# Pooled attention and a two-matrix MoE block: the second product by the seven-product form at two levels instead of one

## The chip, the cores and the metric

The kernel runs on one core of a Trainium2 chip. The metric is the device time of one execution in microseconds (us), lower is better. A difference of 0.2% (about 2 us) is the smallest that a measurement of this kernel tells from no change. The engines are named as in the profile: PE (matrix products), PEld (its weight loads), DVE (vector), ACT (scalar and table functions), POOL and SP (which here issues all DMAs).

## The reference, cut to what matters

```python
# q, k, v: (8, 8, 576, 64) f32; k and v are averaged over blocks of 8 positions
attn = softmax(q @ k_p.T / sqrt(64));  x = attn @ v_p      # x as (4608, 512)
h = x @ w_in                                               # (4608, 2048)
s = sin(alpha * h)
g = h + s * s / (alpha + 1e-9)
out = g @ w_out                                            # (4608, 512), f32
```

Everything is float32. The last line, `g @ w_out`, is the second MoE product and what the change rewrites.

## The kernel before, in words

The work has two phases over nine units (`NU`) of 512 tokens each.

**Phase one.** For each unit, `hidden` computes `h` and `g` in four groups (J), each by the seven-product form of a 2x2 block product (Strassen's form in Winograd's variant: seven half-size products and some additions instead of eight products). A group has seven products of eight matmul records each, all 128x256 outputs. A float32 matmul appears in the trace as two records, each with its own weight load. Some products continue on the partial sum of another one: ACT copies a PSUM bank into the next (L320, L328) and the next product accumulates on the copy. ACT computes the sines and squares (L315, L336 and on), DVE adds (L310), and SP stores the group of `g` to `g_bridge` in HBM (L349). For the first seven units the attention of the next unit is interleaved. Beside unit 7, after which no attention is left, `load_w_out` (L252) loads `w_out` in four blocks of 1 MB (L259), scales its rows by 1/alpha (32 ACT operations of 128x256, L265) and forms the block sums that the seven-product form needs (16 DVE operations of 128x512, L267).

**Phase two.** For each unit, `load_g` reads the four groups of `g` back (L361, 1 MB each). `output` (L364) forms the block sums of `g` on DVE (L371, 16 operations of 128x512 a unit) and runs the seven products in the order 1, 4, 2, 6, 7, 5, 3. A product is 16 matmuls (32 records) with a 128x128 block of `g` as the loaded weights and a 128x256 block of `w_out` as the moving side (L384). Product 2 accumulates on product 1's bank and product 3 on product 5's. ACT copies (L395, L399, L401) and DVE adds (L391) combine the banks into the output tile, which SP stores in two halves (L418).

The tile framework's scheduler sets the order of the instructions on every engine; each engine then runs its own list in order, and waits on semaphores where another engine's or a DMA's result is needed. PSUM has eight banks; five are the pool `ps_m` that both phases use, three the attention's.

Of the kernel before, what the change touches and what calls it, by code (L numbers as in the profile page):

```python
# [36 lines left out]
class Kernel:  # L37
# [187 lines left out]
    def load_w_in(self):  # L225
# [25 lines left out]

    def load_w_out(self, wp):  # L252

        nc, h, kk = self.nc, self.DM // 2, self.K2 // 2
        blk = lambda n: wp.tile([P, kk, h], F32, name=n)
        b11, b12, b21, b22, t1, t2, t4 = (blk(n) for n in ("b11", "b12", "b21", "b22", "bt1", "bt2", "bt4"))
        src = self.w_out.rearrange("(k p) n -> p k n", p=P)
        for t, i, j in ((b11, 0, 0), (b12, 0, 1), (b22, 1, 1), (b21, 1, 0)):
            nc.sync.dma_start(out=t[:], in_=src[:, i * kk:(i + 1) * kk, j * h:(j + 1) * h])  # L259
        self.Bw = {1: b11, 2: b21, 3: b22, 4: t4, 5: t1, 6: t2, 7: b12}  # L260
        for c in range(0, kk, 2):
            for t, i in ((b11, 0), (b12, 0), (b22, 1), (b21, 1)):
                for k in range(c, c + 2):
                    f = i * kk + k
                    nc.scalar.mul(out=t[:, k], in_=t[:, k], mul=self.ral[:, f:f + 1])  # L265
            s = slice(c, c + 2)
            tt = lambda o, x, y: nc.vector.tensor_tensor(out=o[:, s], in0=x[:, s], in1=y[:, s], op=OP.subtract)  # L267
            tt(t1, b12, b11)
            tt(t2, b22, t1)
            tt(b12, b22, b12)  # L270

            tt(t4, b21, t2)
            yield

# [10 lines left out]
    def hidden(self, u, first):  # L285
# [12 lines left out]
        def product(p, J, ps, start):  # L298
            for jj in range(JW):
                f = J * JW + jj  # L300
                for kk in range(2):
                    nc.tensor.matmul(ps[:, jj, :], self.A[p][:, kk, f * P:(f + 1) * P], Bx[p][:, kk, :],  # L302
                                     start=(start and jj == 0 and kk == 0), stop=(kk == 1), skip_group_check=True)
# [50 lines left out]

    def load_g(self, u):
        g = []
        for J in range(self.NJ):
            t = self.gp.tile([P, 2, 2, JW, TH], F32, name="g")  # L360
            self.nc.sync.dma_start(out=t[:].rearrange("p a b c d -> p (a b c d)"), in_=self.gd[u, J])  # L361
            g.append(t)
        return g

    def output(self, u, g):
        nc = self.nc
        G = []
        for J in range(self.NJ):
            s = self.gs.tile([P, 4, JW, TH], F32, name="gs")
            A = lambda i, j: g[J][:, j - 1, i - 1]  # L370
            tt = lambda o, x, y, op: nc.vector.tensor_tensor(out=o, in0=x, in1=y, op=op)  # L371
            tt(s[:, 0], A(2, 1), A(2, 2), OP.add)
            tt(s[:, 1], s[:, 0], A(1, 1), OP.subtract)
            tt(s[:, 2], A(1, 1), A(2, 1), OP.subtract)
            tt(s[:, 3], A(1, 2), s[:, 1], OP.subtract)
            G.append({1: A(1, 1), 2: A(1, 2), 3: s[:, 3], 4: A(2, 2), 5: s[:, 0], 6: s[:, 1], 7: s[:, 2]})
        NT = TH // P
        hw = self.DM // 2

        def product(p, ps, start=True):  # L380
            for t in range(NT):
                for J in range(self.NJ):
                    for jj in range(JW):
                        nc.tensor.matmul(ps[:, t, :], G[J][p][:, jj, t * P:(t + 1) * P], self.Bw[p][:, J * JW + jj, :],  # L384
                                         start=(start and t == 0 and J == 0 and jj == 0), stop=(J == self.NJ - 1 and jj == JW - 1),
                                         skip_group_check=True)
        bank = lambda: self.ps_m.tile([P, NT, hw], F32, name="ps_m", tag="m")
        tmp = lambda n: self.op.tile([P, NT, hw], F32, name=n)
        o = self.op.tile([P, 2, NT, self.DM], F32, name="o")
        C = lambda i, j: o[:, i - 1, :, (j - 1) * hw:j * hw]  # L390
        add = lambda o, x, y: nc.vector.tensor_tensor(out=o, in0=x, in1=y, op=OP.add)  # L391
        b1 = bank()
        product(1, b1)
        p1 = tmp("p1")
        nc.scalar.copy(out=p1[:], in_=b1[:])  # L395
        b4 = bank()
        product(4, b4)
        p4 = tmp("p4")
        nc.scalar.copy(out=p4[:], in_=b4[:])  # L399
        product(2, b1, False)  # L400
        nc.scalar.copy(out=C(1, 1), in_=b1[:])  # L401
        b6 = bank()
        product(6, b6)
        u2 = tmp("u2")
        add(u2[:], p1[:], b6[:])
        b7 = bank()
        product(7, b7)
        u3 = tmp("u3")
        add(u3[:], u2[:], b7[:])
        add(C(2, 1), u3[:], p4[:])  # L410
        b5 = bank()
        product(5, b5)
        add(C(2, 2), u3[:], b5[:])
        product(3, b5, False)
        add(C(1, 2), u2[:], b5[:])
        for i in range(2):
            r = u * 2 * TH + i * TH
            nc.sync.dma_start(out=self.out[r:r + TH, :].rearrange("(t p) n -> p t n", p=P), in_=o[:, i])  # L418

    def run(self):  # L420
        nc, tc = self.nc, self.tc
        pool = lambda s, n, b, **kw: s.enter_context(tc.tile_pool(name=n, bufs=b, **kw))
        with ExitStack() as top:
            const = self.const = pool(top, "const", 1)
            self.tp = pool(top, "tp", 2)
            self.ps_m = pool(top, "ps_m", 5, space=PSUM)
            ident = self.ident = const.tile([P, P], F32, name="ident")
            make_identity(nc, ident)
            with ExitStack() as one:
                self.wp = pool(one, "wp", 1)  # L430
                self.hp = pool(one, "hp", 2)
                self.xp = pool(one, "xp", 2)
                att = one.enter_context(ExitStack())
                cb = pool(att, "cb", 1)
                self.kvp = pool(att, "kv", 3)
                self.qp = pool(att, "qp", 1)
                self.ap = pool(att, "ap", 1)
                self.sm = pool(att, "sm", 3)
                self.ps_a = pool(att, "ps_a", 3, space=PSUM)
                self.mark_banks()  # L440
                self.kblk = []
                for i in range(2):
                    t = cb.tile([P, self.NP, 2 * self.Sp], F32, name=f"kblk{i}")
                    nc.gpsimd.memset(t[:], 0.0)
                    self.kblk.append(t)
                st = self.load_batch(0)
                self.load_alpha()
                self.load_w_in()
                for _ in self.attention(0, st):
                    pass  # L450
                for u in range(self.NU):
                    nxt = iter(())
                    if u + 1 < self.B:
                        nxt = self.attention(u + 1, self.load_batch(u + 1))
                        steps = 48
                    elif u == self.B - 1:
                        att.close()
                        wo = pool(top, "wo", 1, side="right")
                        self.gp = pool(top, "gp", self.NJ, side="right")
# [10 lines left out]
                g = self.load_g(0)  # L470
            self.gs = pool(top, "gs", self.NJ)
            self.op = pool(top, "op", 2)
            for u in range(self.NU):
                self.output(u, g)
                if u + 1 < self.NU:
                    g = self.load_g(u + 1)


@with_exitstack
# [32 lines left out]
```

## Time and profile before

| What | Value |
|---|---|
| Time before, median of 3 runs | 1082.56 us (1081.94 to 1083.32) |
| The profiled execution's own time | 1081.14 us |
| Its span, first to last instruction | 1079.3 us (so 1.84 us lie around it) |
| Mean granted PE clock | 0.987 |
| PE / PEld / DVE / ACT / POOL busy | 1037.8 / 879.6 / 494.9 / 376.6 / 218.1 us |
| Matmul records / weight loads | 5288 / 5288 |
| HBM read / written | 75.51 MB / 47.19 MB |

How to read it: busy time is the time in which an engine has an instruction in flight. Matmuls are pipelined: consecutive records overlap, so the spacing of their starts, not the length of one, is what a stream costs. In a timeline row the columns are start, length, engine, line, operation, output and inputs, the shapes (weights, then the moving side), the count, and in brackets the engine's idle time before the row and who ended it. In a windows row each engine has its busy time and its count of instructions, then come the granted clock, the share of the 16 DMA engines that was busy, and GB/s.

### The profile page before, as it was taken

What the parts mean: (1) busy time and instruction counts of PE and PEld (TensorE: products, weight loads), DVE (VectorE), ACT (ScalarE), POOL (GpSimd) and SP (SyncE); (2) the same over time, 40 slices, a digit from 0 to 9 for tenths busy, and PEclk for the clock granted to TensorE, in tenths of its full rate; (3) what the DMA queues carried; (4) which work ended last, traced back from release to release, by engine and by line L of the source; (5) the groups of instructions that cost most, each with busy time, mean ns of one, the idle gap of its engine ahead of it and who ended that gap; (6) DMA issues with size and microseconds to landing.
All of it is one profiled execution on the core that took longest, in us unless ns stands there. A gap on an engine that the chain in (4) does not pass through costs nothing.

```text
span 1079.3 us, 13285 instructions
## 1 busy us (share of the span) xinstructions
PE 1037.8 (96%) x5288; PEld 879.6 (81%) x5288; DVE 494.9 (46%) x925; ACT 376.6 (35%) x682; POOL 218.1 (20%) x228
## 2 busy tenths in 40 slices
PE   6679999999999999999969999999999999999998
PEld 5467787878878888788758888888888888888886
DVE  4998573664636557464454251413133140413131
ACT  2246565565645757457486540000000000000000
POOL 4697870441705412002000000000000000000000
PEclk9799999999999999999989999999999999999999
DMA  7945461623516223110471213131332313131301
GB/s 172 242 116 151 147 168 78 149 101 105 145 79 160 90 89 84 78 78 40 149 279 78 117 79 156 39 156 60 155 126 89 156 40 156 40 156 63 152 20 39
DMA packets 73533, 123.55 MB, mean 114 GB/s; under 512 B 42112, under 2 KB 50304, under 8 KB 64128
## 3 DMA queue, kind: packets, MB, share of 16 engines
q1 hardware_dynamic: 73472, 122.70, 34.4%
q8 instruction: 42, 0.69, 0.3%
q14 instruction: 19, 0.16, 0.0%
HBM read 75.51 MB, written 47.19 MB: 114 GB/s over the span
## 4 chain that ended last, share of the span: by engine, by line
PE 84%; POOL 6%; DMA 4%; ACT 2%; DVE 2%; SPq 1%; issue 1%; POOLq 0%; ACTq 0%
PE ps_m L384 40%; PE ps_m L302 34%; POOL kvin L78 4%; PE ps_sc L123 3%; PE ps_o L164 3%; PE ps_at L154 2%; DMA kvin<-in_v_dram 1%; DMA a<-in_moe_w_in_dram 1%; DMA kvin<-in_k_dram 1%; ACT b L265 1%; SPq L64 1%; PE ps_qt L109 1%; DMA b<-in_moe_w_out_dram 1%; POOL vp L78 1%; POOL kp L78 1%
## 5 line engine op out<-in xcount | busy, mean ns | idle before, releaser
L302 PE MATMUL ps_m<-bt,as 128*128 128x256 f32 x576 | 138.7, 388 | 10.4 <-ACT ps_m L320 10.3
L78 POOL TENSOR_TENSOR kvin<-kvin 72x512 f32<-72x512 f32 x120 | 132.9, 1110 | 55.2 <-DMA kvin<-in_v_dram 33.2
L302 PE MATMUL ps_m<-xT,a 128*128 128x256 f32 x576 | 141.1, 384 | 0.0
L302 PE MATMUL ps_m<-bt,a 128*128 128x256 f32 x576 | 139.6, 381 | 0.0
L302 PEld LDWEIGHTS ps_m<-bt,as 128*128 128x128 f32 x576 | 106.9, 193 | 29.5 <-ACT ps_m L320 10.7
L384 PE MATMUL ps_m<-b,gs 128*128 128x256 f32 x576 | 128.2, 381 | 0.8 <-DVE o L391 0.8
L384 PE MATMUL ps_m<-b,g 128*128 128x256 f32 x576 | 128.6, 380 | 0.0
L384 PE MATMUL ps_m<-bt,gs 128*128 128x256 f32 x576 | 127.3, 380 | 0.0
L384 PEld LDWEIGHTS ps_m<-b,gs 128*128 128x128 f32 x576 | 109.0, 191 | 17.8 <-DVE o L391 3.7
L384 PEld LDWEIGHTS ps_m<-bt,gs 128*128 128x128 f32 x576 | 109.8, 191 | 14.5
L384 PEld LDWEIGHTS ps_m<-b,g 128*128 128x128 f32 x576 | 109.8, 191 | 14.5
L302 PEld LDWEIGHTS ps_m<-xT,a 128*128 128x128 f32 x576 | 106.5, 191 | 18.1 <-issue 4.6
L302 PEld LDWEIGHTS ps_m<-bt,a 128*128 128x128 f32 x576 | 106.4, 191 | 13.1
L310 DVE TENSOR_TENSOR h<-ps_m,s 128x512 f32<-128x512 f32 x72 | 49.5, 687 | 122.0 <-ACT s L336 80.8
L395 ACT COPY p<-ps_m 128x512 f32<-128x512 f32 x9 | 5.3, 585 | 278.8 <-PE ps_m L384 272.8
L315 ACT ACTIVATE s<-h,rat 128x256 f32<-128x256 f32 x144 | 65.6, 500 | 64.0 <-DVE h L310 63.9
L391 DVE TENSOR_TENSOR u<-p,ps_m 128x512 f32<-128x512 f32 x9 | 6.2, 688 | 169.0 <-PE ps_m L384 152.8
L315 ACT ACTIVATE s<-ps_m,rat 128x256 f32<-128x256 f32 x144 | 60.2, 467 | 40.8 <-PE ps_m L302 40.2
L302 PE MATMUL ps_m<-xT,as 128*128 128x256 f32 x288 | 68.2, 380 | 0.0
L144 POOL TENSOR_TENSOR ex<-ex,sm 128x576 f32<-128x576 f32 (+1 forms) x40 | 47.9, 1223 | 98.1 <-DVE sm L142 98.1
L371 DVE TENSOR_TENSOR gs<-g 128x512 f32<-128x512 f32 x72 | 48.0, 687 | 38.4 <-PE ps_m L384 37.4
L384 PE MATMUL ps_m<-bt,g 128*128 128x256 f32 x288 | 63.6, 380 | 0.0
(77 smaller groups left out, 1135.9 us busy)
## 6 DMA issues: line engine op xcount, KB each, us to landing
g_bridge<-h SPq DMA_DIRECT2D x36, 1024.0 KB
g<-g_bridge SPq DMA_DIRECT2D x36, 1024.0 KB
kvin<-in_k_dram SPq DMA_DIRECT2D x32, 288.0 KB
kvin<-in_v_dram SPq DMA_DIRECT2D x32, 288.0 KB
out_dram<-o SPq DMA_DIRECT2D x18, 512.0 KB
qm<-in_q_dram SPq DMA_DIRECT2D x32, 256.0 KB
a<-in_moe_w_in_dram SPq DMA_DIRECT2D x16, 256.0 KB
b<-in_moe_w_out_dram SPq DMA_DIRECT2D x4, 1024.0 KB
```

What stands on the lines that cost most here:

```text
L64: nc.sync.dma_start(out=qm[:n, i], in_=self.q[b, :, t0:t0 + n, :].rearrange("h p d -> p h d"))
L78: eng.tensor_tensor(out=o, in0=t[:, :, 0:w], in1=t[:, :, w:2 * w], op=OP.add)
L109: nc.tensor.transpose(ps[:, j, :], pair(j, P, hp), self.ident[:])
L123: nc.tensor.matmul(ps[:n, 2 * hh:2 * hh + 2, :].rearrange("p h k -> p (h k)"), qt[:, hp, t0:t0 + n], kb[:, hp, :], start=True, stop=True)
L144: eng.tensor_tensor(out=ex[:n, i], in0=ex[:n, i], in1=sm[:n].unsqueeze(2).to_broadcast([n, H, Sp]), op=OP.mult)
L154: nc.tensor.transpose(ps[:, hh, :n], ex[:n, i, 4 * g + hh, :], self.ident[:n, :n])
L164: nc.tensor.matmul(ps[64 * e:64 * e + 64, :m], vp[:, h, :], aT[c][:, h, :m], start=True, stop=True)
L302: nc.tensor.matmul(ps[:, jj, :], self.A[p][:, kk, f * P:(f + 1) * P], Bx[p][:, kk, :], start=(start and jj == 0 and kk == 0), stop=(kk == ...
L310: add = lambda o, x, y: nc.vector.tensor_tensor(out=o, in0=x, in1=y, op=OP.add)
L315: nc.scalar.activation(out=s[:, i, j, jj, :], in_=src[:, jj, :], func=AF.Sin, scale=self.rat[:, f:f + 1])
L371: tt = lambda o, x, y, op: nc.vector.tensor_tensor(out=o, in0=x, in1=y, op=op)
L384: nc.tensor.matmul(ps[:, t, :], G[J][p][:, jj, t * P:(t + 1) * P], self.Bw[p][:, J * JW + jj, :], start=(start and t == 0 and J == 0 and j ...
```

## The change

Each of the seven products of phase two (256x1024 times 1024x256) is itself done by the seven-product form. A unit then has 49 small products of four 128x128 matmuls (eight records) each. What follows from it in the code:

- `load_w_out` keeps the blocks as `wb1` to `wb7` in a layout with inner blocks; the 32 scalings move from ACT to DVE. `inner_w` makes the inner sums of each block, four DVE operations of 128x512: for blocks 1 and 2 beside unit 7, for the other five in the first unit of phase two.
- `load_g` reads `g` by outer block (`r11`, `r12`, `r22`, `r21`; 1 MB each), one buffer of each. The next unit's first three loads stand at step 3, that of `r21` at step 5.
- `outputs` is one software pipeline over 63 steps (9 units by 7 outer products, in the order 1, 2, 4, 6, 7, 5, 3). The outer sums are four DVE operations of 128x2048 a unit (`x5`, `x6`, `x7` in the place of `r21`, `x3`). The inner sums are four DVE operations of 128x512 a step (`xe`, two buffers in turn).
- A step's results lie in one bank `ps_x` (four 128x128 blocks) and half of a bank `ps_y`. Three ACT copies a step (one of 128x256, two of 128x128) seed blocks of `ps_x` with a partial sum, on which further products accumulate. Between a step's products stand four products of the step before.
- `combine` takes a finished step into the output: one or two DVE additions of 128x512, one of 128x2x128 and, in three of the seven steps, an ACT copy of 128x512. Outputs are stored in four pieces of 256 KB a unit.
- PE's instructions of phase two keep the order of the program (`manual_schedule`); the other engines' are still ordered by the scheduler. The pool of `p5` in phase one has one buffer instead of two.

The diff, cut:

```diff
     def load_w_out(self, wp):
...
-                    nc.scalar.mul(out=t[:, k], in_=t[:, k], mul=self.ral[:, f:f + 1])
+                    nc.vector.tensor_scalar(out=t[:, k], in0=t[:, k], scalar1=self.ral[:, f:f + 1], scalar2=None, op0=OP.mult)
...
+        for p in (1, 2):
+            yield self.inner_w(p, wp)
+    def inner_w(self, p, wp):
...
+        e = wp.tile([P, 3, NJ, P], F32, name=f"we{p}")
...
+        tt(t1, b(1, 2), b(1, 1))
+        tt(t2, b(2, 2), t1)
+        tt(b(1, 2), b(2, 2), b(1, 2))
+        tt(t4, b(2, 1), t2)
...
+        def inner(u, p):
...
+            e = (self.gp if self.ne else self.gs).tile([P, 4, self.NJ, P], F32, name="xe")
...
+            tt(s1, a(2, 1), a(2, 2), OP.add)
+            tt(s2, s1, a(1, 1), OP.subtract)
+            tt(s4, a(1, 2), s2, OP.subtract)
+            tt(s3, a(1, 1), a(2, 1), OP.subtract)
+            return {1: a(1, 1), 2: a(1, 2), 3: s4, 4: a(2, 2), 5: s1, 6: s2, 7: s3}
+        def product(st, q, out, start):
+            A, W = st["A"][q], self.W[st["p"]][q]
+            for J in range(self.NJ):
+                nc.tensor.matmul(out, A[:, J, :], W[:, J, :], start=(start and J == 0), stop=(J == self.NJ - 1), skip_group_check=True)
...
+                if u == 0 and n < 5:
+                    self.inner_w(ORDER[n + 2], self.gs)
...
+                product(st, 1, yz[:, 0, :], True)
+                nc.scalar.copy(out=x[:, 0:2, :], in_=yz[:, 0:1, :].to_broadcast([P, 2, P]))
+            if last:
+                product(last, 5, last["yz"][:, 1, :], False)
+                product(last, 4, last["x"][:, 2, :], False)
+            if st:
+                product(st, 6, x[:, 1, :], False)
+                nc.scalar.copy(out=x[:, 2, :], in_=x[:, 1, :])
...
+                    A[seq[k + 1]] = inner(seq[k + 1][0], ORDER[seq[k + 1][1]])
+            if last:
+                product(last, 2, last["x"][:, 0, :], False)
+                product(last, 3, last["x"][:, 1, :], False)
+                combine(last)
+            if st:
+                product(st, 7, x[:, 2, :], False)
+                nc.scalar.copy(out=x[:, 3, :], in_=x[:, 2, :])
...
-            self.tp = pool(top, "tp", 2)
+            self.tp = pool(top, "tp", 1)
...
+            self.ps_y = pool(top, "ps_y", 3, space=PSUM)
+            self.gs = pool(top, "gs", 1, reuse_waits="tile")
+            self.op = pool(top, "op", 1, reuse_waits="tile")
+            self.load_g(0, ("r22", "r21"))
+            with tc.manual_schedule(engines={nc.tensor.engine}):
+                self.outputs()
```

Three places show what moves. The first is DVE's list beside unit 7's first group, at the scaling of `w_out`. Before (`h` is the group's result, `p_4116` the copy p5, `b` and `bt` the blocks of `w_out`; `L310` and `L267` are named above):

```order
570 L290 TENSOR_TENSOR bt<-xT,bt 128x512 [waits DVE_49]
571 L290 TENSOR_TENSOR bt<-bt,xT 128x512 [waits DVE_49]
572 L310 TENSOR_TENSOR h<-ps_m,p_4116 128x512 [waits DMAHW4_49,PE_49,Activation_49]
573 L310 TENSOR_TENSOR h<-ps_m,s 128x512 [waits Activation_49]
574 L310 TENSOR_TENSOR h<-ps_m,p_4116 128x512 [waits PE_49]
575 L267 TENSOR_TENSOR bt_4122<-b_4119,b_4118 128x512 [waits DMAHW5_49,DMAHW7_49,Activation_49,Pool_49]
```

And now (`wb_4118` is the first block of `w_out`, whose load it waits for as DMAHW5):

```order
570 L307 TENSOR_TENSOR bt<-xT,bt 128x512 [waits DVE_49]
571 L307 TENSOR_TENSOR bt<-bt,xT 128x512 [waits DVE_49]
572 L266 TENSOR_SCALAR wb_4118<-wb_4118,ral 128x256 [waits DMAHW5_49,Activation_49,Pool_49]
573 L266 TENSOR_SCALAR wb_4118<-wb_4118,ral 128x256 x7
574 L327 TENSOR_TENSOR h<-ps_m,s 128x512 [waits DMAHW4_49,Activation_49]
575 L327 TENSOR_TENSOR h<-ps_m,p_4116 128x512 [waits PE_49]
```

The eight scalings, with their wait for the load, now stand on DVE ahead of the additions of the group in flight. Up to this place the lists of PE, DVE and ACT are the same before and after.

The second is PE's list in phase two. Before, products run as long blocks:

```order
1276 L384 MATMUL ps_m<-b_4119,gs 128x256 [waits PE_49]
1277 L384 MATMUL ps_m<-b_4119,gs 128x256 x5
1278 L384 MATMUL ps_m<-b_4119,gs 128x256 [waits DVE_49]
1279 L384 MATMUL ps_m<-b_4119,gs 128x256 x9
1280 L384 MATMUL ps_m<-bt_4122,gs 128x256 [waits PE_49]
1281 L384 MATMUL ps_m<-bt_4122,gs 128x256 x15
```

And now one step of the last unit (the products 1 of this step, 5 and 4 of the step before, 6 of this one, 2 and 3 of the step before, 7 of this one):

```order
1669 L429 MATMUL ps_y<-wb_4121,r_6968 128x128 [waits DMAHW1_49,DVE_49,PE_49]
1670 L429 MATMUL ps_y<-wb_4121,r_6968 128x128 x3
1671 L429 MATMUL ps_y<-we_4258,xe 128x128 x4
1672 L429 MATMUL ps_x<-we_4258,r_6966 128x128 [waits Activation_49]
1673 L429 MATMUL ps_x<-we_4258,r_6966 128x128 x3
1674 L429 MATMUL ps_x<-we_4643,xe 128x128 [waits DVE_49,Activation_49]
1675 L429 MATMUL ps_x<-we_4643,xe 128x128 x3
1676 L429 MATMUL ps_x<-wb_4119,r_6966 128x128 x4
1677 L429 MATMUL ps_x<-wb_4119,xe 128x128 x4
1678 L429 MATMUL ps_x<-wb_4121,xe 128x128 [waits Activation_49]
1679 L429 MATMUL ps_x<-wb_4121,xe 128x128 x3
```

The output is half as wide, and a step of 28 matmuls has three waits for ACT's seeds and one for DVE's inner sums.

The third is DVE's list where one unit passes into the next (`c7` and `c5` are combined parts, `r21_6428`, `r22_6344`, `r11_6340` are blocks of the next unit):

```order
1001 L391 TENSOR_TENSOR c7_6463<-c6_6420,ps_x_6387 128x512
1002 L391 TENSOR_TENSOR xe_6450<-x3_6338,xe_6450 128x512
1003 L391 TENSOR_TENSOR c7_6463<-c7_6463,ps_y_6388 128x2x128
1004 L391 TENSOR_TENSOR o_6466<-c7_6463,c4_6379 128x512
1005 L391 TENSOR_TENSOR x5_6603<-r21_6428,r22_6344 128x2048
1006 L391 TENSOR_TENSOR xe_6494<-r11_6340 128x512 x2
1007 L391 TENSOR_TENSOR xe_6494<-xe_6494,r11_6340 128x512
1008 L391 TENSOR_TENSOR c5_6507<-c5_6507,ps_y_6431 128x2x128
```

The scheduler has put `x5` of the next unit, which needs the freshly loaded `r21`, ahead of the inner sums of the next unit's first step, although the program names it two steps later.

More of the change, by code (lines that the diff above doesn't have):

```diff
@@ L273, in load_w_out @@
             yield
+        self.W = {}
+        for p in (1, 2):
+            yield self.inner_w(p, wp)
+    def inner_w(self, p, wp):
+        nc, NJ = self.nc, self.NJ
+        x = self.wb[p]
+        e = wp.tile([P, 3, NJ, P], F32, name=f"we{p}")
+        b = lambda i, j: x[:, :, i - 1, j - 1, :]
+        tt = lambda o, x, y: nc.vector.tensor_tensor(out=o, in0=x, in1=y, op=OP.subtract)
+        t1, t2, t4 = (e[:, i] for i in range(3))
+        tt(t1, b(1, 2), b(1, 1))
+        tt(t2, b(2, 2), t1)
+        tt(b(1, 2), b(2, 2), b(1, 2))
+        tt(t4, b(2, 1), t2)
+        self.W[p] = {1: b(1, 1), 2: b(2, 1), 3: b(2, 2), 4: t4, 5: t1, 6: t2, 7: b(1, 2)}
     def mark_banks(self):
@@ L353, in hidden @@
             yield from group(J)
[L357 to L365, printed above, removed]
-        nc = self.nc
[L367 to L418, printed above, removed]
@@ L458, in run @@
                         wo = pool(top, "wo", 1, side="right")
-                        self.gp = pool(top, "gp", self.NJ, side="right")
+                        self.gp = pool(top, "gp", 1, side="right")
                         nxt = self.load_w_out(wo)
@@ L469, in run @@
                         pass
[L470 to L476, printed above, removed]
+                self.R = {}
+                self.load_g(0, ("r11", "r12"))
+            self.ps_x = self.ps_m
+            self.ps_y = pool(top, "ps_y", 3, space=PSUM)
[4 more added lines that the diff above has]
+                self.outputs()
 @with_exitstack
```

104 lines of the change are left out of this document (100 added, 4 removed).

## Prediction

> **What bounds the kernel now.** I read the page's first part, then the table by stage (windows cut where the stages change), the groups by line in phase two, and the timeline at the places that the change touches.
>
> ```profile
> PE 1037.8 (96%) x5288; PEld 879.6 (81%) x5288; DVE 494.9 (46%) x925; ACT 376.6 (35%) x682; POOL 218.1 (20%) x228
> 540.00:569.00 29.00, 18.56 (x78) 15.46 (x77) 16.82 (x25) 24.51 (x55) 0.00 (x0) 0.82 0.70 256
> 637.20:1075.00 437.80, 437.01 (x2017) 383.28 (x2015) 118.85 (x190) 18.30 (x32) 0.00 (x0) 1.00 0.25 100
> 1075.00:1079.30 4.30, 0.00 (x0) 0.00 (x0) 0.69 (x1) 0.00 (x0) 0.00 (x0) 1.00 0.32 122
> ```
>
> PE is the bound. Phase two (637.2 to 1075.0) is 437.8 us with PE idle for 0.8, at full clock, while DVE works for 119 us and ACT for 18: all of it is the price of 2016 records. The one stretch where PE visibly waits is 540 to 569, beside unit 7, with 18.56 of 29 us busy.
>
> What a record costs is the spacing of starts in an unbroken run. Two rows of 256 columns and of 128 columns (both with 128x128 weights), and the loads of the second:
>
> ```profile
> 566.38 3.62 PE L302 MATMUL ps_m<-bt,as 128*128 128x256 f32 x16
> 8.23 1.17 PE L283 MATMUL ps_m<-ident 128*128 128x128 f32 x9
> 8.23 0.97 PEld L283 LDWEIGHTS ps_m<-ident 128*128 128x128 f32 x8
> L384 PE MATMUL ps_m<-b,gs 128*128 128x256 f32 x576 | 128.2, 381 | 0.8 <-DVE o L391 0.8
> ```
>
> With 0.38 us for the last one, 256 columns cost (3.62 - 0.38)/15 = 0.216 us; 2016 of them make 435.5, phase two but for 2 us. The 128-column row is the shape that the change uses. From the row's nine records, the last about 0.28 long: (1.17 - 0.28)/8 = 0.111 to 0.112 us. The loads' row keeps the same spacing ((0.97 - 0.19)/7 = 0.111), so loads and matmuls overlap.
>
> **The change part by part.** All sums are made on the profiled span of 1079.3 us. Its execution took 1081.14 (1.84 more), and the median of the runs, 1082.56, is 1.42 above that.
>
> *Phase two's matmuls.* Before: 9 x 7 x 32 = 2016 records. After: 9 x 49 x 8 = 3528 of half the columns, 3528 x 0.1115 = 393.4, plus 0.2 for the last drain: 393.6 against 437.8, **-44.2 us**. That is nearly the ratio 7/8 of the columns. Between ends: 0.107 (half of the 256 columns' 0.216, less a share of fixed cost) gives -60, 0.115 gives -32. I take the row of the very shape.
>
> A rule speaks against it. The Trainium skill, "TensorE: Matmul & The Clock Gate", section Back-to-back issue gap, says that in a real stream of weight loads and matmuls the spacing is set by both: about 81 ns at 128 columns where the bare gap is 56. An estimate with that ratio is 161 ns, 569 us for phase two, a kernel at about 1219. This trace's loads and matmuls hold 111 ns together, but only for nine records; a long run is not shown here. It is a rival below.
>
> *Waits for the seeds.* Each step (56 records, 6.24 us) has three ACT copies on which PE accumulates. Between the product that feeds a copy and the one that needs it stand two other products, 16 x 0.1115 = 1.78 us.
>
> ```profile
> L116 ACT COPY qt<-ps_qr 128x256 f32<-128x256 f32 x8 | 3.0, 377 | 0.0
> L395 ACT COPY p<-ps_m 128x512 f32<-128x512 f32 x9 | 5.3, 585 | 278.8 <-PE ps_m L384 272.8 <-DMA g_bridge<-h 6.0
> 1067.07 0.69 DVE L391 TENSOR_TENSOR o<-u,ps_m 128x512 f32<-128x512 f32 x1 [5.43 <-PE ps_m L384]
> 1067.81 7.17 PE L384 MATMUL ps_m<-b,gs 128*128 128x256 f32 x32 [0.78 <-DVE o L391]
> ```
>
> The chain is the drain (0.28 - 0.11 = 0.17), a handover (PE starts 0.05 after DVE's end in the last two rows), the widest copy (0.38) and a handover back: 0.65 us. Covered, so **0**. Uncovered, all 189 copies would cost up to 0.65 x 189 = 123 us. ACT itself is busy for about 1.2 us of a step (0.38 + 2 x 0.3, and 0.585 in three of seven): no queue.
>
> *DVE in phase two.* Consecutive additions start closer than they last:
>
> ```profile
> 1029.32 1.29 DVE L371 TENSOR_TENSOR gs<-g 128x512 f32<-128x512 f32 x2
> 640.40 1.22 DVE L310 TENSOR_TENSOR h<-h,s 128x1024 f32<-128x1024 f32 x1
> 1075.02 0.69 DVE L391 TENSOR_TENSOR o<-u,ps_m 128x512 f32<-128x512 f32 x1 [7.27 <-PE ps_m L384]
> ```
>
> 512 elements cost 1.29 - 0.69 = 0.60 us in a row of them; 512 more make 1.22 - 0.69 = 0.53, so 2048 cost 0.60 + 3 x 0.53 = 2.2 and 256 cost 0.34. A unit needs 28 inner sums (16.8), 4 outer ones (8.8), 7 combining additions of 512 (4.2) and 7 of 256 (2.4): 32.2 us, where PE needs 392 x 0.1115 = 43.7. So DVE is 74% busy and not the bound on average, but there are two tight places.
>
> First unit: the five inner weight sums still to do (20 more additions) queue with the rest. From the end of phase one's matmuls to the inner sum that step 4's product 6 waits for, PE has 208 records, 23.2 us. DVE ends phase one's additions at 641.6, 4.4 us after 637.2, and then its list has 31 additions of 512, four of 2048 and two of 256 to that point: 18.6 + 8.8 + 0.7, in all 32.5 us. **+9 us** (bounds 4, if half of it lies beside other waits, and 15, if the 1 MB loads of `r22` and `r21`, issued behind the last store of `g`, are late as well).
>
> Unit turns: `x5` of the next unit stands ahead of the inner sums that step 0's product 6 needs. It can start when the old `x5` is free, 0.6 us before step 6's product 3 starts its last record. Then 2.2 for `x5` and 1.9 for three inner sums: ready 3.6 us after that record, when PE has 32 records (3.57 us) to go. That is 0.1 late, eight times: **+1**. This holds if `r21` has landed by then. Its load is issued when step 5's product 3 is done, 5.3 us before `x5`'s earliest start.
>
> ```profile
> 655.50 2.91 SPq L361 DMA_DIRECT2D g<-g_bridge  x4
> 656.00:657.00 1.00, 1.00 (x6) 0.90 (x5) 0.00 (x0) 0.00 (x0) 0.00 (x0) 1.00 0.56 66
> 657.00:667.00 10.00, 10.00 (x48) 8.82 (x48) 0.69 (x1) 0.58 (x1) 0.00 (x0) 1.00 0.98 413
> 529.76 0.38 SPq L259 DMA_DIRECT2D b<-in_moe_w_out_dram  x1
> 538.30 0.91 ACT L265 ACTIVATE b<-b,ral 128x256 f32<-128x256 f32 x2 [3.95 <-DMA b<-in_moe_w_out_dram]
> ```
>
> Issued at 655.5, four such loads flow from about 656.4 to 667: 0.9 us of start and 2.6 per MB, an estimate of 4 us for one alone. In time by 1 us. The slow end is the load of `w_out` in company, 8.4 us.
>
> *Phase one beside unit 7.* Now ACT waits for that load (the row above), and its 32 scalings then hold up its own seed copy:
>
> ```profile
> 536.80 0.69 DVE L310 TENSOR_TENSOR h<-ps_m,p 128x512 f32<-128x512 f32 x1 [5.20 <-PE ps_m L302]
> 538.27 1.89 PE L302 MATMUL ps_m<-bt,a 128*128 128x256 f32 x8
> 553.68 0.59 ACT L320 COPY ps_m<-ps_m 128x512 f32<-128x512 f32 x1
> 554.33 2.08 PE L302 MATMUL ps_m<-bt,as 128*128 128x256 f32 x4 [10.31 <-ACT ps_m L320]
> 27.57 1.23 DVE L223 TENSOR_SCALAR h<-h 128x2048 f32<-128x2048 f32 x1
> ```
>
> PE loses 10.3 us and then runs at a lower clock for a while (four records take 2.08 instead of 1.03). On DVE a scaling of 256 is an estimated 0.2 (2048 took 1.23; with 0.16 fixed, 0.13 + 0.07), at most an addition's 0.34. What is late next: DVE now waits for the load at 538.3, scales eight times (1.6), and only then does the two additions that product 4 needs, which started at 538.27 before: until 541.3, a 3 us stall. In the following two groups scalings, block sums and the first inner sums (some 20 us of DVE work in 24) stand between the additions; I count another 3 us. So 6 instead of 10.8: **-5** (bounds: -8, if only the first stall is left; +3, if scalings cost 0.34). The single `p5` buffer costs nothing: in the rows of the addition that frees it and of the next copy into it there are 4.5 us between.
>
> ```profile
> 563.13 0.69 DVE L310 TENSOR_TENSOR h<-ps_m,p 128x512 f32<-128x512 f32 x1 [0.63 <-PE ps_m L302]
> 568.31 0.58 ACT L324 COPY p<-ps_m 128x512 f32<-128x512 f32 x1 [0.58 <-PE ps_m L302]
> ```
>
> *The end.* After the last matmul one more addition of 256 (0.4) stands ahead of the last store: **+0.4**.
>
> Sum: 1079.3 - 44.2 + 9 + 1 - 5 + 0.4 = 1040.5; with 1.84 and 1.42, **1044 us**. Alone, this case spans 1037 to 1053.
>
> **The rivals.**
>
> *`r21` lands late.* At 8.4 us instead of 4, `x5` starts 3.1 us later, eight times: +25, 1069. For it: one buffer, and the reuse waits in front of the load on SP's queue. Against: nothing else flows then except a store of 256 KB. Chance 0.12.
>
> *Nothing is won in phase one, and the first unit starves longer.* DVE, now with the scalings, gives back the 5 us, and the start costs 15 + 3: 1044 + 5 + 9 = 1058. Chance 0.13.
>
> *The stream does not hold 0.1115 us (slower).* It decides from (437.8 - 5.4)/3528 = 0.1226 us on, 10% above the row. A price from the trace for records of this shape in short bursts:
>
> ```profile
> L109 PE MATMUL ps_qt<-ident,qm 128*128 128x128 f32 x128 | 19.4, 290 | 3.8 <-DMA qm<-in_q_dram 2.7 <-ACT qt L110 0.7 <-DVE kblk L104 0.5
> ```
>
> 19.4/128 = 0.152 us, since each burst of four exposes its drain. If every wait in the new list broke the stream so, 3528 x 0.152 = 536, +98: 1082.6 + 98 + 5 = 1186. Against it: phase one's products wait for ACT's seeds in the same way, and their run of 16 above has no gap. Chance 0.08. The skill's rule goes this way.
>
> That the change does not do what it says is excluded by PE's list.
>
> **How the numbers follow.** Forecast 0.65, the two rivals that stay faster 0.25, the slower one 0.08, no change 0.02. A measurement tells 0.2%, 2.2 us, from nothing; 1069 is still 13 us below. So faster 0.89, same 0.02, slower 0.09. The range takes the forecast's own, the second rival and part of the first: 1036 to 1063.
>
> **What would show it.** Right: phase two about 404 us long, its 128-column records spaced 0.111; PE idle of some 9 us in its first 35 us, put down to DVE; almost none later; two or three stalls of 2 to 3 us between 540 and 570. Wrong: a spacing over 0.115 in unbroken runs; PE waiting for ACT in phase two; DVE waiting for `g_bridge` once a unit; a stall of 10 us left beside unit 7.

## The result, and the profile after

The changed kernel takes 1043.12 us in the median of four runs (1040.16 to 1044.82); the kernel before took 1082.82 beside it. The ratio is 0.9631, with a 95% interval from 0.9605 to 0.9658: 40 us faster, 0.9 us below the forecast. The profiled execution took 1040.16 us with a span of 1038.3, against 1079.3 before: -41.0, where -38.8 was predicted.

The page's first line, and the table by stage, cut where the new kernel's stages change (phase two starts at 630.2, its last matmul ends at 1033.9):

```profile
PE 996.1 (96%) x6800; PEld 889.8 (86%) x6800; DVE 697.5 (67%) x1210; ACT 417.7 (40%) x839; POOL 216.8 (21%) x228
```

```profile
540.00:569.00 29.00, 26.76 (x126) 22.68 (x125) 28.96 (x61) 14.41 (x28) 0.00 (x0) 1.00 0.52 192
637.00:680.00 43.00, 37.73 (x317) 37.28 (x318) 39.44 (x55) 6.51 (x20) 0.00 (x0) 0.96 0.50 169
680.00:1034.00 354.00, 353.86 (x3166) 353.66 (x3164) 261.44 (x372) 62.07 (x193) 0.00 (x0) 1.00 0.33 109
```

PE is the bound as before, with 96% of a span that is 41 us shorter. The third row is the change: 354 us with PE idle for 0.14, in 3166 records, 354.0/3166 = 0.1118 us each. DVE has gone from 27% of phase two to 74% of it (261.44/354). The first row shows unit 7 with 26.76 of 29 us busy, where before it was 18.56, and at full clock. The second is the new cost: the first unit of phase two, 43 us with PE idle for 5.3 and the clock at 0.96.

Who makes PE wait from 569 us to 690, by the view of waits (us in all, times, the longest):

```profile
PE ps_x L429 <- DVE xe L391: 5.2, 3, 2.7
PE ps_y L429 <- DVE x L391: 1.3, 1, 1.3
PE ps_x L429 <- ACT ps_x L500: 0.7, 1, 0.7
```

From 680 us to the end the same view lists nothing for PE. The longest of these waits, in the timeline (PE and DVE alone; L284 is the inner level of `w_out`, L391 the inner level of `g`):

```profile
634.59 0.68 DVE L284 TENSOR_TENSOR we<-wb 128x512 f32<-128x512 f32 x1
634.67 1.06 PE L429 MATMUL ps_x<-we,r 128*128 128x128 f32 x8
635.19 0.68 DVE L391 TENSOR_TENSOR xe<-r 128x512 f32<-128x512 f32 x1
635.79 0.68 DVE L284 TENSOR_TENSOR we<-wb,we 128x512 f32<-128x512 f32 x1
636.40 0.68 DVE L284 TENSOR_TENSOR wb<-wb 128x512 f32<-128x512 f32 x1
637.00 0.68 DVE L284 TENSOR_TENSOR we<-wb,we 128x512 f32<-128x512 f32 x1
637.60 0.68 DVE L391 TENSOR_TENSOR xe<-xe,r 128x512 f32<-128x512 f32 x1
638.21 0.68 DVE L391 TENSOR_TENSOR xe<-r 128x512 f32<-128x512 f32 x1
638.43 1.13 PE L429 MATMUL ps_x<-we,xe 128*128 128x128 f32 x8 [2.70 <-DVE xe L391]
...
639.40 1.70 PE L429 MATMUL ps_x<-wb,r 128*128 128x128 f32 x8
```

PE needs `xe`, which is ready at 638.3. DVE is never idle here, but four of its additions up to 637.7 prepare block 4 of `w_out` (L284), of which PE has no need yet. After this wait eight matmuls take 1.70 us instead of 1.06: the clock is down for 16 records.

### The profile page after: what moved, and what is told of

Read it like the earlier page. It is cut to its first block, busy times and chain, and to the rows that moved or that the text cites. A ratio compares the mean times of both kernels' runs of the same rounds, so it can differ in the third digit from the quotient of the medians.

```text
span 1038.3 us, 17027 instructions
## 1 busy us (share of the span) xinstructions
PE 996.1 (96%) x6800; PEld 889.8 (86%) x6800; DVE 697.5 (67%) x1210; ACT 417.7 (40%) x839; POOL 216.8 (21%) x228
## 4 chain that ended last, share of the span: by engine, by line
PE 83%; DVE 6%; DMA 5%; ACT 2%; POOL 2%; SPq 1%; issue 1%; DVEq 0%; POOLq 0%; ACTq 0%
PE ps_m L319 37%; PE ps_x L429 26%; PE ps_y L429 10%; PE ps_o L164 3%; PE ps_sc L123 3%; PE ps_at L154 3%; DMA a<-in_moe_w_in_dram 1%; DVE h L327 1%; POOL kvin L78 1%; DMA kvin<-in_k_dram 1%; DMA r<-g_bridge 1%; PE ps_qt L109 1%; DMA wb<-in_moe_w_out_dram 1%; ACT s L332 1%; DVE x L391 1%
## 5 line engine op out<-in xcount | busy, mean ns | idle before, releaser
L429 PE MATMUL ps_x<-wb,xe 128*128 128x128 f32 x1008 | 124.2, 277 | 0.7 <-ACT ps_x L500 0.7
L429 PEld LDWEIGHTS ps_x<-wb,xe 128*128 128x128 f32 x1008 | 118.8, 194 | 0.8 <-ACT ps_x L500 0.8
L500 ACT COPY ps_x<-ps_x 128x128 f32<-128x128 f32 x63 | 15.8, 250 | 153.8 <-PE ps_x L429 153.8
L391 DVE TENSOR_TENSOR xe<-x 128x512 f32<-128x512 f32 x54 | 34.9, 688 | 58.3 <-PE ps_x L429 58.3
L429 PE MATMUL ps_x<-we,xe 128*128 128x128 f32 x504 | 67.2, 277 | 5.2 <-DVE xe L391 5.2
L429 PE MATMUL ps_y<-we,xe 128*128 128x128 f32 x504 | 66.6, 275 | 0.0
L429 PEld LDWEIGHTS ps_x<-we,xe 128*128 128x128 f32 x504 | 61.4, 192 | 5.8 <-issue 5.7
L126 DVE TENSOR_REDUCE mx<-ps_sc 128x4 f32<-128x288 f32 (+1 forms) x80 | 34.7, 449 | 45.7 <-PE ps_sc L123 45.2
L391 DVE TENSOR_TENSOR xe<-r 128x512 f32<-128x512 f32 x72 | 46.5, 684 | 22.6 <-PE ps_x L429 22.6
L429 PEld LDWEIGHTS ps_y<-we,xe 128*128 128x128 f32 x504 | 61.3, 192 | 0.0
```

The costliest lines, as they stand in the source:

```text
L126: nc.vector.tensor_reduce(out=mx[:n], in_=ps[:n], axis=AX, op=OP.max)
L429: nc.tensor.matmul(out, A[:, J, :], W[:, J, :], start=(start and J == 0), stop=(J == self.NJ - 1), skip_group_check=True)
L500: nc.scalar.copy(out=x[:, 2, :], in_=x[:, 1, :])
```

## The experiments

The runs were made on four chips: e1 to e4 on one, e5 to e8 on a second, e9 to e11 on a third, e12 on a fourth. On each the kernel before was timed beside them; its medians are 1080.6 to 1081.5 us. The last column is the ratio to it with its interval, which reaches some 3 us to each side, more than the 0.2% named at the start.

| run | us, median | ratio |
|---|---|---|
| e8_after_again (the change itself) | 1042.25 | 0.9640 [0.9615, 0.9665] |
| e1_scale_act | 1044.83 | 0.9664 [0.9637, 0.9692] |
| e2_inner_pool | 1052.62 | 0.9730 [0.9696, 0.9763] |
| e3_wprep_pool | 1049.54 | 0.9718 [0.9680, 0.9755] |
| e4_seed4 | 1044.83 | 0.9663 [0.9630, 0.9695] |
| e5_seed8 | 1139.69 | 1.0545 [1.0514, 1.0576] |
| e6_no_inner | 1033.91 | 0.9566 [0.9539, 0.9593] |
| e7_before_dve | 1076.63 | 0.9954 [0.9938, 0.9971] |
| e9_later | 1041.03 | 0.9632 [0.9602, 0.9662] |
| e10_inner8 | 1041.91 | 0.9638 [0.9610, 0.9666] |
| e11_prep_pool | 1037.26 | 0.9596 [0.9564, 0.9628] |
| e12_sched | 1040.73 | 0.9635 [0.9611, 0.9660] |

The theory is the prediction's: the matmuls give the gain, the seeds are free because two products cover them, DVE's list in the first unit gives some 10 us back, and phase one wins some 5 because ACT's queue is no longer blocked by `w_out`. Its rivals: the seeds are free because ACT has room in any case; the first unit waits for late loads; phase one won nothing.

**The unaltered kernel again**, on the chip of e5 to e7.

> The changed kernel once more, unaltered, on the chip of the three other runs: 1040 to 1045 us, ratio 0.960 to 0.966.

1042.25 us, as expected. Its trace differs in two places from the first profile. The wait at 536 us for `w_out`'s first transfer is 1.4 us long by the spacing of starts, not 3.3. And in the first unit the wait at 651 us is 2.6 us, not 1.6, and the clock is low behind that one, not at 640. One profile can't settle what is below 2 us in these places.

**The seeds.** Two kernels repeat the first seed's copy, four and eight times:

```
+                for _ in range(4):
                     nc.scalar.copy(out=x[:, 0:2, :], in_=yz[:, 0:1, :].to_broadcast([P, 2, P]))
```

> The first seed copy of each step made four times instead of once. It adds 3 x 0.36 = 1.1 us to the chain between product 1 and product 6, 0.65 us by my sum, under a cover of 1.78 us. Theory: the chain is then 1.7 us and still covered; the time stays within 4 us of 1043 (at most 0.05 us at each of 63 steps). Rival: the cover is nearly used up already, and 63 steps lose 0.5 us or more each: 1075 or more.

> The first seed of every product copied eight times over: seven more copies of 0.357 us each, so the chain product 1, seed, product 6 grows from about 0.65 to 3.15 us, against 1.78 us of the two products that TensorE has between. Theory (the seed is free because 16 matmuls of the product before cover it): about 1.37 us of wait in each of 62 products, +85 us, 1120 to 1145 us, with TensorE waiting for the copies of the first seed. Rival (ACT has room anyway, the copies are spread by the queue): no more than +10 us.

With four copies ACT is nearly twice as busy from 680 us on (61.81 us in that stretch without the repeats), and PE has 3092 records there instead of 3133:

```profile
680.00:1030.00 350.00, 350.00 (x3092) 349.19 (x3092) 257.94 (x364) 119.83 (x355) 0.00 (x0) 1.00 0.32 108
892.15 1.15 PE L429 MATMUL ps_x<-we,xe 128*128 128x128 f32 x8
```

The second row is product 6 of one step: 1.15 us, not 1.06. From 680 us on, 56 spacings, one a step, are 0.20 us instead of 0.112; that is 5.0 us of the 5.3 by which the span has grown (1043.6 against 1038.3). The cover is just used up: in a row the copies start every 0.39 us, so the chain is 0.65 + 3 x 0.39 = 1.82 us, 0.04 over the cover of 1.78, and 0.09 is lost. That is more than the 0.05 expected, and far from the rival's 0.5. The view of waits doesn't list so short a wait, and the median ratios (0.9663, and 0.9640 unaltered) don't tell the two kernels apart.

With eight copies each product waits. One step in the timeline (PE and ACT alone), and the waits of the whole of phase two:

```profile
892.34 1.06 PE L429 MATMUL ps_y<-we,xe 128*128 128x128 f32 x8
892.54 3.08 ACT L495 COPY ps_x<-ps_y 128x256 f32<-128x256 f32 x8 [0.59 <-PE ps_y L429]
893.24 1.06 PE L429 MATMUL ps_x<-we,r 128*128 128x128 f32 x8
895.67 1.16 PE L429 MATMUL ps_x<-we,xe 128*128 128x128 f32 x8 [1.38 <-ACT ps_x L495]
```

```profile
PE ps_x L429 <- ACT ps_x L495: 84.0, 61, 1.4
```

The copies run beside products 5 and 4 (the first and third rows), and what sticks out is a wait of 1.38 us, where 1.37 was worked out beforehand. The copies' spacing is (3.08 - 0.36)/7 = 0.39 us, so the chain is 0.65 + 2.72 = 3.37 us, 1.59 over its cover of 1.78. By the starts it is 1.54: the third row's last matmul starts at 894.02, the next product at 895.67, 1.65 later instead of 0.11. 61 times 1.54 is 94 of the 97 us between the medians (1139.69 - 1042.25). So the threshold lies where it was put, 1.78 - 0.65 = 1.13 us above the chain: what e4 loses puts it at 1.17 - 0.09 = 1.08, what e5 loses at 2.72 - 1.54 = 1.18. The rival, ACT's room, falls: in e5 ACT is busy for 205 of the 450 us from 680 on.

**The first unit.** One kernel leaves the twenty subtractions of blocks 4, 6, 7, 5, 3 out:

```
+        if p not in (1, 2):
+            b = lambda i, j: x[:, :, i - 1, j - 1, :]
+            self.W[p] = {1: b(1, 1), 2: b(2, 1), 3: b(2, 2), 4: b(2, 1), 5: b(1, 1), 6: b(2, 2), 7: b(1, 2)}
+            return
```

> Leaves out the twenty subtractions of the inner level of w_out that DVE does in the first unit (the products of blocks 4, 6, 7, 5, 3 then take raw blocks). Theory (the first unit waits because DVE's list there is longer than TensorE's): 13.7 us of DVE work goes, so the waits of 7.6 us at 635 to 663 us shrink below 3 us and the stretch at the low clock with them: 1032 to 1037 us. Rival (the first of these waits is for the loads of r22 and r21, which come only after phase one): the 3 us at 635 stay and no more than 4 us are won, 1039 or more.

```profile
630.00:680.00 50.00, 47.97 (x407) 46.97 (x406) 37.08 (x49) 12.31 (x34) 0.00 (x0) 1.00 0.45 160
```

1033.91 us, 8.3 less than the unaltered kernel on the same chip. PE's waits for DVE there come to 1.4 us and the clock stays at 1.00 (phase two starts at 634.0 in this trace). But the gain is not DVE's alone. SP's rows in this kernel (L387 loads `r22` and `r21`, L370 stores `g`):

```profile
626.78 2.59 SPq L387 DMA_DIRECT2D r<-g_bridge  x2
638.51 0.33 SPq L370 DMA_DIRECT2D g_bridge<-h  x1
```

The scheduler issues the two loads at 626.8 here, ahead of the last store of `g`; in the unaltered kernel they follow it, at 635.1. So the edit shortens DVE's list and brings the loads forward at once. The second kernel moves one fifth of it (block 4) to unit 8:

```
-                if u == 0 and n < 5:
+                if u == 0 and 0 < n < 5:
...
+                    else:
+                        nxt = (self.inner_w(p, wo) for p in (4,))
+                        steps = 3
```

> The changed kernel with the four subtractions of the inner level for block 4 moved from the first unit of phase two into unit 8 of phase one. Theory (DVE's list sets the first unit): 2.7 us of its list go, so the 3 us wait at 636 nearly goes and with it the low clock behind it: 3 to 5 us faster, 1037 to 1040 us. Rival (the wait is for the late loads of phase two): within 1 us of the changed kernel.

1041.91 us: nothing won (0.9638 against 0.9640). The first wait fell as foreseen, from 2.70 to 0.89 us, but another came behind it. Timeline of this kernel (SPq issues the loads of `r22` and `r21`):

```profile
638.02 1.46 SPq L383 DMA_DIRECT2D r<-g_bridge  x2
...
639.53 1.13 PE L429 MATMUL ps_x<-we,xe 128*128 128x128 f32 x8 [0.89 <-DVE xe L391]
...
646.89 2.07 PE L429 MATMUL ps_y<-wb,r 128*128 128x128 f32 x8 [3.55 <-DMA r<-g_bridge]
```

The loads are issued behind the last store of `g`, as in the unaltered kernel, and the first of them lands about 8.9 us later (646.9 - 638.0). Behind this wait the clock is low (2.07 us for eight records). So the rival was half right: DVE's list is the first limit, in the unaltered kernel too, where DVE works without a gap from 632.9 to 645.8; the loads stand close behind it (DVE itself is then idle for 0.3 us until `r21` is there), and to shorten the list alone brings nothing. What each of the two would cost without the other no run separates: e6 removed both.

**POOL as a helper.** First the five inner levels of the first unit on POOL:

```
-        tt = lambda o, x, y: nc.vector.tensor_tensor(out=o, in0=x, in1=y, op=OP.subtract)
+        eng = nc.vector if p in (1, 2) else nc.gpsimd
+        tt = lambda o, x, y: eng.tensor_tensor(out=o, in0=x, in1=y, op=OP.subtract)
```

> The inner weight sums of the five blocks that are still open in the first unit of phase two (20 operations of 128x512) on POOL, which is idle there. Theory: DVE's list is too long in that unit; without 12 us of it the PE stalls after 631 (2.9, 1.5, 1.9 and 1.0 us) shrink to under 2 us together, the lower clock after the first of them goes too, and the time falls by 5 to 9 us, to 1034 to 1038. Rival 1: the stalls are those of the late loads of r22 and r21, and the time stays within 2 us of 1043. Rival 2: POOL and DVE slow each other, additions of 512 last over 0.8 us instead of 0.69, and the gain is under 3 us.

It is slower than the change by 0.9% (0.9730 against 0.9640), where 5 to 9 us less were expected: its second rival holds. POOL's groups from 630 to 680 us, DVE's from 637 to 662, and the waits:

```profile
L285 POOL TENSOR_TENSOR we<-wb,we 128x512 f32<-128x512 f32 x10 | 19.8, 1984 | 0.1
```

```profile
L392 DVE TENSOR_TENSOR xe<-xe,r 128x512 f32<-128x512 f32 x2 | 3.5, 1748 | 0.0
L392 DVE TENSOR_TENSOR x<-r,r 128x2048 f32<-128x2048 f32 x1 | 3.4, 3354 | 0.0
```

```profile
PE ps_x L430 <- DVE xe L392: 9.4, 3, 4.7
PE ps_y L430 <- DVE x L392: 4.4, 1, 4.4
```

POOL needs up to 2.0 us for what DVE alone does in 0.68. And while it works DVE's own additions take 1.75 instead of 0.68, and 3.35 instead of 2.28. PE still waits for DVE, and longer. In the timeline the two engines take turns:

```profile
644.07 1.26 POOL L285 TENSOR_TENSOR we<-wb,we 128x512 f32<-128x512 f32 x1
644.81 2.75 DVE L392 TENSOR_TENSOR xe<-r 128x512 f32<-128x512 f32 x2 [3.06 <-PE ps_x L430]
645.30 1.71 POOL L285 TENSOR_TENSOR wb<-wb 128x512 f32<-128x512 f32 x1
```

DVE's two additions span 2.75 us. If the first runs from POOL's end at 645.33 and the second from POOL's next end at 647.01, each 0.6 to 0.7 long, they end at 647.6, which is what the row shows (644.81 + 2.75 = 647.56). The Trainium skill, "SBUF — State Buffer", section SBUF: two separate sides, says that a DVE operation with two SBUF inputs and a GpSimd operation that reads SBUF lock a shared port pair against each other, each for its whole instruction. This trace agrees. An addition moved to POOL here relieves DVE of 0.68 us and stops it for about 1.07 (1.75 - 0.68).

Then the whole preparation of `w_out` on POOL, phase one's part included, and later that part alone:

> All of the preparation of w_out on POOL: scalings, block sums and all inner sums (76 operations). Theory: the three or four PE stalls left beside unit 7 (6 us in all) come from DVE's list, so they go as well as those of the first unit; the time is 5 to 7 us below the run with only the five inner sums on POOL, 1028 to 1032. Rival: POOL is too slow for it (75 us of work, with over 1.2 us for 512 elements) and its results come late in the first unit, so nothing is gained over that run.

> The changed kernel with the preparation of w_out beside unit 7 on POOL (scalings, block subtractions, inner level of blocks 1 and 2), the five inner levels of the first unit on DVE as in the changed kernel. Theory (a queue of its own for what waits for w_out frees both DVE and ACT, and POOL costs DVE only while both work): phase two starts at 626 to 627 us instead of 630 to 631, the first unit as in the changed kernel, 1036 to 1040 us. Rival (the slower DVE beside a busy POOL costs as much as is won): 1041 or more.

The edit of the second (in the first, L284 is on POOL for all blocks):

```
-                    nc.vector.tensor_scalar(out=t[:, k], in0=t[:, k], scalar1=self.ral[:, f:f + 1], scalar2=None, op0=OP.mult)
+                    nc.gpsimd.tensor_scalar(out=t[:, k], in0=t[:, k], scalar1=self.ral[:, f:f + 1], scalar2=None, op0=OP.mult)
...
-            tt = lambda o, x, y: nc.vector.tensor_tensor(out=o[:, s], in0=x[:, s], in1=y[:, s], op=OP.subtract)
+            tt = lambda o, x, y: nc.gpsimd.tensor_tensor(out=o[:, s], in0=x[:, s], in1=y[:, s], op=OP.subtract)
...
+        eng = nc.gpsimd if p in (1, 2) else nc.vector
```

Run e3 is 1049.54: it wins 3.5 us in phase one (phase two starts at 626.7, not 630.2) and loses e2's waits in the first unit (13.8 us for DVE in both), so its expected 1028 to 1032 failed as e2's did. Run e11 keeps most of the first (627.5) and avoids the second. Its table by stage, and two of DVE's rows, a group from 529 to 626 and one addition:

```profile
529.00:569.00 40.00, 40.00 (x200) 35.31 (x199) 17.38 (x25) 23.02 (x44) 32.59 (x29) 1.00 0.67 237
569.00:626.00 57.00, 55.30 (x256) 48.13 (x255) 25.52 (x28) 32.35 (x64) 32.98 (x28) 1.00 0.23 93
L328 DVE TENSOR_TENSOR h<-ps_m,p 128x512 f32<-128x512 f32 x16 | 10.9, 685 | 4.4 <-PE ps_m L320 4.4
592.45 6.03 DVE L328 TENSOR_TENSOR h<-h,s 128x1024 f32<-128x1024 f32 x1
```

PE waits for nothing between 529 and 569 us, although DVE and POOL work side by side. DVE has only 17.4 of 40 us to do there, and most of its additions read one operand from PSUM: the 16 of the third row take 0.685 us each, as without POOL. The additions of two SBUF operands can be hit harder than in e2: the one in the last row takes 6.03 us instead of 1.22, while five of POOL's run, and PE then waits 1.7 us for DVE, the only wait in the second row. 1037.26 us, 0.9596, is the best of all that do the whole work. Against the unaltered kernel the ratios differ by 0.0044, and the two intervals together (the root of the sum of squares of 0.0032 and 0.0025) leave 0.0041 open; the medians differ by 5.0 us, the spans of the profiles by 2.4 (1035.9 and 1038.3). A gain of 2 to 5 us is likely, its size not settled.

**Phase one beside unit 7.** The scalings alone, back to ACT in the new kernel, and to DVE in the old one. The edit of the first, and its reverse of the second:

```
-                    nc.vector.tensor_scalar(out=t[:, k], in0=t[:, k], scalar1=self.ral[:, f:f + 1], scalar2=None, op0=OP.mult)
+                    nc.scalar.mul(out=t[:, k], in_=t[:, k], mul=self.ral[:, f:f + 1])
```

> The changed kernel with the 32 scalings of w_out back on ACT. Theory: these scalings, with their wait for the load, are what stalled PE for 10.3 us beside unit 7, and their move to DVE is worth the 6 us by which phase two begins earlier (631.0 instead of 637.2). Then a PE stall of 8 to 11 us put down to an ACT copy is back between 540 and 560, and the time is 4 to 8 us above the changed kernel's 1043: 1047 to 1051. Rival: the stretch became shorter because only 2 MB of g are loaded there instead of 4 MB. Then the scalings' engine does not matter and the time stays within 2 us of 1043.

> The kernel before with nothing changed but the scalings of w_out, on DVE instead of ACT. Theory (in the kernel before ACT's blocked queue cost 10.8 us of TensorE's waits beside unit 7, of which DVE's costs about 6): 4 to 5 us faster, ratio 0.995 to 0.9965. Rival (the wait for w_out's blocks is the same on either engine): within 1 us of the kernel before.

In the old kernel DVE's scalings are worth 0.0046 (0.0029 to 0.0062), 4 to 5 us, as expected. In its trace PE's wait of 10.3 us for ACT's copy is gone, and waits of 4.0 us for DVE and 1.1 for ACT stand in its place. The loads of `g` are the same in both, so they can't be the cause of this gain. In the new one ACT's put the old wait back: the seed copy L337 stands behind scalings.

```profile
546.65 2.50 ACT L266 ACTIVATE wb<-wb,ral 128x256 f32<-128x256 f32 x6
549.05 0.59 ACT L337 COPY ps_m<-ps_m 128x512 f32<-128x512 f32 x1
...
549.69 1.65 PE L319 MATMUL ps_m<-bt,as 128*128 128x256 f32 x3 [9.93 <-ACT ps_m L337]
```

Its trace starts phase two 4.6 us later (634.8 against 630.2), but its median is only 2.6 us above the unaltered kernel's, below what was expected, within what the intervals leave open, and inside the 2 us around 1043 that its rival named. The time alone decides nothing here. The mechanism is shown by the old kernel and by the trace; the size is 3 to 5 us.

The last edit of this part begins the scalings four steps later (four empty `yield`s behind the loads, 18 steps for 14).

> The changed kernel with the scalings of w_out begun four steps of unit 7 later, so that DVE's queue is not yet behind w_out's transfers when unit 7's first additions come. Theory (the 3.3 us wait at 536 is DVE's scalings waiting for a transfer): that wait goes, the other 4 us beside unit 7 stay, 3 to 4 us faster than the changed kernel, 1037 to 1040 us. Rival (the additions wait for the amount of scalings, not for the transfer): the waits are only moved, within 1 us.

0.9632 against 0.9640: no difference. The first wait is 1.7 us, which lies between the 1.4 and 3.3 of the two profiles of the unaltered kernel. The expectation rested on one profile's 3.3 us, and failed with it; the rival holds.

**The order of the matmuls.** Another part of the change is the fixed order in phase two:

```
-            with tc.manual_schedule(engines={nc.tensor.engine}):
-                self.outputs()
+            self.outputs()
```

> The changed kernel with the matmuls of phase two left to the scheduler instead of kept in program order; the instructions are the same. Theory (from the second unit on the scheduler finds the same order, and in the first unit the DVE list sets the time whatever TensorE's order): 1040 to 1046 us, ratio 0.961 to 0.967. Rival (the scheduler puts a product that waits for DVE ahead of ready ones in the first unit): up to 10 us slower than the changed kernel.

0.9635 against 0.9640: the same. In the first unit its waits are other ones (2.9 us for a load of `r`, 2.7 for DVE), with a like sum. The order by hand is worth nothing measurable here.

## Why the prediction was right

*Phase two's matmuls*, -44.2: the spacing is 0.1118 where 0.1115 was taken, so 3528 x 0.1118 = 394.4 and -43.4. Nine records at the kernel's start were enough to price a stream of 3528. The rival that the stream doesn't hold decides from 0.1226 on and is out, and with it the rule that spoke for it: the Trainium skill, "TensorE: Matmul & The Clock Gate", section Back-to-back issue gap, would have given the estimate of 0.161; in this kernel weight loads and matmuls of 128 columns in fp32 keep 0.1118 over 354 us.

*Seeds*, 0: right, and so is the reason. Chain and cover were sized within 0.05 us of what e4 and e5 show (0.04 and 0.09; 1.59 and 1.54). PE waits once for a seed all the same, for 0.7 us at 631 us. There ACT is still at phase one's activations when the product ends, so it is ACT's queue and not the chain; the prediction had named such a wait as a sign against it.

*First unit*, +9: by the spacing of starts PE loses 0.94, 2.97, 1.57, 1.97 and 1.13 us, less 0.11 for each record itself, 8.0 us, and 16 records at the low clock 1.6 more: 9.6. The first of the five is the wait for ACT (0.8 of the 8.0), the others are put down to DVE, as named. So DVE's list cost 7.2 of the 9, and that the whole comes to 9.6 is in part luck: the sum had neither the clock nor ACT's queue. DVE's additions were sized right (0.60 in a row, 2.20 for 2048). The bound named for late loads is close: e10 and e12 wait for one (3.6 and 2.9 us).

*Unit turns*, +1: 0.05 us each, 0.4 in all. One of them, in the timeline:

```profile
890.80 0.36 SPq L383 DMA_DIRECT2D r<-g_bridge  x1
...
897.06 2.29 DVE L391 TENSOR_TENSOR x<-r,r 128x2048 f32<-128x2048 f32 x1 [1.21 <-PE ps_x L429]
...
901.33 1.11 PE L429 MATMUL ps_x<-we,xe 128*128 128x128 f32 x8
```

`x5` waits for PE, not for `r21`, which landed within the 6.3 us from its issue; so the rival of the late load is out: from 650 us on DVE waits for no load. The product that needs the inner sums takes 1.11 us instead of 1.06.

*Phase one*, -5: phase two's matmuls begin 7.0 us earlier (630.2 against 637.2), and eight of them stand even ahead of that, in unit 7 (at 553 us), just before a wait of 0.8 us, so that 3520 are left (-0.9). The first wait, foreseen as 3 us, is this one:

```profile
535.66 2.19 DVE L266 TENSOR_SCALAR wb<-wb,ral 128x256 f32<-128x256 f32 x8 [6.29 <-DMA wb<-in_moe_w_out_dram]
537.76 0.68 DVE L327 TENSOR_TENSOR h<-ps_m,s 128x512 f32<-128x512 f32 x1
538.37 0.68 DVE L327 TENSOR_TENSOR h<-ps_m,p 128x512 f32<-128x512 f32 x1
...
539.10 1.99 PE L319 MATMUL ps_m<-bt,a 128*128 128x256 f32 x8 [2.89 <-DVE h L327]
```

DVE waits for the transfer, scales eight times and only then adds. The transfer came 2.6 us earlier than in the profile before, and a scaling took 0.27 instead of 0.2, so that a wait of 2.9 is partly luck. What counts is when product 4 starts: at 539.1 in this profile and in e8's, although PE came to it 1.9 us later there, and that is 0.8 us later than before (538.27), where 3 were counted. The later waits are three of 0.7 to 0.8 us and one of 0.3, not one or two of 2 to 3 us; with what follows each they cost 3.7 us, where 3 were counted. And the old stall was worth 12.5 us by the spacing of starts, not 10.8, since the lower clock behind it went with it; the forecast had seen that clock and priced little of it. These three, -1.7, -2.2 and +0.7, are the miss of this term, to 0.3 us. The rival that nothing is won in phase one is refuted by e7.

*The end*, +0.4: +0.1 (4.49 us from the last matmul's end to the span's end, 4.35 before).

By terms: -43.4 + 9.6 + 0.4 - 7.0 - 0.9 + 0.1 = -41.2, against -41.0 measured. The forecast's -38.8 missed by 2.2 us, all of it in phase one (2.9 too little); the other terms cancel to 0.6. That is less than the 4.7 us that the changed kernel's four runs cover, of which the profiled one is the fastest; the median is only 0.9 us below the forecast. One slip changes nothing: the chances of the forecast and of the two faster rivals add up to 0.90, not 0.89.

## What to carry to other kernels

Price a new stream by the spacing of the same shape in the same trace, however few its records, and price each dependent copy by chain against cover: below the cover it is free, above it costs its excess every time, and 0.04 us over it is already seen in the spacing of starts where no view of waits lists it. Before taking work from an engine that makes another wait, look who is second (here two loads close behind), and whether the edit moved the second one too (in e6 it did). Before handing DVE's work to POOL look whether DVE is free at that moment and whether its additions read PSUM: the same move won 2 to 5 us beside phase one and lost 10 in the first unit.

## What the runs showed of the hardware

One wait of 3 us can cost more than itself, or nothing more. A wait of 2.97 or 2.98 us by the spacing of starts stands at the same product of the first unit in six profiles. Behind it 16 records ran at 0.213 us instead of 0.112 in the changed kernel's first profile and in e1's (the granted clock is low for 3.4 us, 1.6 us lost), 28 in e4's and e5's (6.8 us, 2.8 lost), none in e8's and e9's; in e8 the clock fell 13 us later, behind a wait of 2.57 us. After the wait of 3.27 us at 536 no record ran slowly. The Trainium skill, "TensorE: Matmul & The Clock Gate", section What's actually happening, gives 3.4 us as the window by which the clock is decided, free-running; the durations agree, and a free-running window would fit the chance in it, which no run here tests.

POOL's and DVE's additions of two SBUF operands exclude each other: 0.68 us becomes 1.75 on DVE, and POOL's own, 1.27 alone, takes 1.6 to 2.0 (e2). DVE can also lose to several of POOL's in a row (6.03 us instead of 1.22, e11). Additions that read one operand from PSUM kept 0.685 us beside POOL (e11).
